# Three more places for expert weights, another order of places, eight PSUM banks for the second half, four row blocks stored by halves

## The chip, the cores and the metric

The kernel runs on one core of a Trainium2 chip. The metric is the device time of one execution in microseconds (us). TensorE (PE) does the matrix products, VectorE (DVE) and ScalarE (ACT) empty PSUM, GpSimd (POOL) does a few element-wise steps, and SyncE (SP) issues every DMA, in one in-order queue.

## The reference, cut to what matters

Three stages in float32: attention over 32 memory slots, a layer that takes the maximum of three products, and a soft mixture of eight experts. Only the last one is touched by the change. Its inputs are the 4608 rows `x` of 512 columns that the second stage leaves.

```python
logits = x @ phi                       # 4608 x 32 slots
d = softmax(logits, axis=0)            # over the rows
slot_input = (d.T @ x).reshape(E, 4, 512)
for e in range(E):                     # E = 8 experts
    h = maximum(slot_input[e] @ w1[e], 0)     # w1[e]: 512 x 1024
    slot_out[e] = h @ w2[e]                   # w2[e]: 1024 x 512
c = softmax(logits, axis=1)            # over the 32 slots
return c @ slot_out.reshape(32, 512)   # 4608 x 512
```

## The kernel before

**The stages.** The list `ORDER` is a hand-written order in which the attention and the second stage of eight batches run, until about 387 us of the span. Then follow the last softmax over the rows and the slot inputs (until about 400 us), the experts' first weights (`ex_in`, from 399.7 us), the experts' second weights by column halves (`ex_out(e, 0)`, then `ex_out(e, 1)`), and the output rows (`st_out`).

**The expert weights.** The weights are cut into 64 pieces of 128 x 1024 floats, 512 KB each. `pieces` lists them in the order of their use: first weights of expert 0, first weights of expert 1, first-half second weights of expert 0, and so on; the last 16 pieces are the second-half second weights of the eight experts. Each piece goes to a *place* in SBUF; `slots` lists the places in the order in which memory comes free, and piece k goes to place k modulo `NSLOT`. `send(n)` issues the DMAs of the next n pieces on SP. Before, `NSLOT` is 41. The first 34 places are spare memory and memory that the attention frees. Three more (`more2`) come free when `main_x` closes at the end of `ORDER`, one in `hbuf` after the last slot sums, three in `wo` after the last product with it. The 23 pieces that are left go to the first 23 places again: `ex_in` and `ex_out` call `send(1)` after each piece that they have used. A place can also be a list of four parts of 256 columns (`mix`), which are loaded by four DMAs of 128 KB.

**The output rows.** There are nine row blocks: block r below 8 holds the first 512 rows of batch r, block 8 the 64 last rows of every batch. `st_out(r, x)` computes columns 256x to 256x+255 of a block: twelve products into four PSUM banks `ts[0..3]`, then four copies to SBUF, two by ACT and two by DVE. The banks come from `mx()`, the pool `x` of four banks; `ps_m` has three further banks and `ps_l` one. First halves (x = 0) run between the `ex_out(e, 1)`, second halves (x = 1) at the end, in the order 0 to 5, 8, 6, 7. The number `NH` decides how a block is stored. Block r below `NH` is stored by halves: each half has a place of its own and one DMA of 512 KB, whose runs in DRAM are 1 KB. The other blocks have two places, both halves are gathered there, and only after the second half two DMAs of 512 KB with runs of 2 KB store them (four of 256 KB from 64 partitions each for block 8). Before, `NH` is 6.

**The DMAs' order.** SP issues the reloads first, in the order of the pieces, and the stores after them, in the order of `st_out`. Each DMA also waits for the one eight places ahead of it in the queue (eight semaphores serve in turn).

**Names.** L286 and L284 are the two `dma_start` lines of `send` (whole piece, part of a piece), L1016 the products of `ex_in`, L1033 those of `ex_out`, L1082 and L1086 those of `st_out`, L1095 and L1093 its copies on ACT and DVE, L1106 the store of a half block, L1099 that of two quarters of a whole block, L1104 that of block 8.

Of the kernel before, what the change touches and what calls it, by code (L numbers as in the profile page):

```python
# [7 lines left out]
FP32 = mybir.dt.float32  # L8
# [17 lines left out]
PIECE = 1024  # L26
NX = 6
# [133 lines left out]
LL = 0  # L161
VP = 3
EXTRA = 2
NSLOT = EXTRA + 9 + 12 + NX + 2 + 3 + 3 + 1 + 3


@with_exitstack
def kernel(
# [18 lines left out]
    ps_m = ctx.enter_context(tc.tile_pool(name="ps_m", bufs=3, space=PSUM))  # L187
    ps_l = ctx.enter_context(tc.tile_pool(name="ps_l", bufs=1, space=PSUM))
# [12 lines left out]
    def bank(pool, tag):  # L201
        return pool.tile([128, 512], FP32, tag=tag, name=tag)

    def mx():
        return bank(ps_x, "x")


    arena = keep.tile([128, (9 + 12 + NX) * PIECE], FP32, name="arena")
# [6 lines left out]
    s_run = keep.tile([128, FF], FP32, name="s_run")  # L215
    stat = keep.tile([128, 2], FP32, name="stat")
    h5x = keep.tile([128, 1920], FP32, name="h5x")
# [6 lines left out]
    hbuf = keep.tile([128, 3, 1536], FP32, name="hbuf")  # L224
# [17 lines left out]
    x0 = a0 + 12288  # L242
# [13 lines left out]
    slots = [extra[:, PIECE * j:PIECE * j + PIECE] for j in range(EXTRA)]  # L256
    slots += [arena[:, o:o + PIECE] for o in slot_off]
    late_slots = [h5x[:, 0:PIECE]] + [arena[:, PIECE * j:PIECE * j + PIECE] for j in range(9)]
    late_slots += [hbuf[:, 2, 0:PIECE], arena[:, x0:x0 + PIECE]]

    order = [("in", 0)]
    for e in range(E):
# [8 lines left out]
    def slot(k):  # L271
        return slots[k % NSLOT]

# [4 lines left out]
    def send(n):  # L278
        for _ in range(n):
            if sent[0] < len(pieces):  # L280
                x = slot(sent[0])
                if isinstance(x, list):
                    for g in range(4):
                        nc.sync.dma_start(out=x[g], in_=pieces[sent[0]][:, 256 * g:256 * g + 256])  # L284
                else:
                    nc.sync.dma_start(out=x, in_=pieces[sent[0]])  # L286
                sent[0] += 1
# [418 lines left out]
    def st_exp(t, rows, key):  # L706
        nm = pair.tile([128, 4], FP32, tag="nm", name="nm")
        rs = slice(0, rows)
        nc.vector.tensor_reduce(out=nm[rs, 0:1], in_=t[rs, 0:128], axis=AX.X, op=ALU.max)
        nc.vector.tensor_scalar(  # L710
            out=nm[rs, 2:3], in0=nm[rs, 0:1], scalar1=stat[rs, 0:1], scalar2=-1.0, op0=ALU.max, op1=ALU.mult)
        nc.vector.tensor_tensor(out=nm[rs, 1:2], in0=stat[rs, 0:1], in1=nm[rs, 2:3], op=ALU.add)
        nc.vector.tensor_scalar(out=stat[rs, 0:1], in0=nm[rs, 2:3], scalar1=-1.0, scalar2=None, op0=ALU.mult)
        dt = pair.tile([128, 128], FP32, tag="dt", name="dt")
        sm = pair.tile([128, 4], FP32, tag="sm", name="sm")
        o, x = dt[rs], t[rs, 0:128]
        if 1 < key < B - 1:
            o, x = o.rearrange("p (t a) -> p a t", a=4), x.rearrange("p (a t) -> p a t", a=4)
        nc.scalar.activation(out=o, in_=x, func=ACTF.Exp, bias=nm[rs, 2:3], accum_out=sm[rs, 1:2])
        nc.scalar.activation(out=sm[rs, 0:1], in_=nm[rs, 1:2], func=ACTF.Exp)  # L720
        nc.vector.scalar_tensor_tensor(
            out=stat[rs, 1:2], in0=stat[rs, 1:2], scalar=sm[rs, 0:1], in1=sm[rs, 1:2],
            op0=ALU.mult, op1=ALU.add)
        nc.scalar.activation(out=lt_all[rs, key], in_=t[rs, 0:128], func=ACTF.Copy)
        dtok[key] = (dt, sm)
# [70 lines left out]
    def warm(n, late=False):  # L796
        if n < 1:
            return
        t = bank(ps_m, "m") if late else bank(ps_l, "l")
        for _ in range(n):  # L800
            nc.tensor.matmul(t[:, 0:128], ident, ident, start=True, stop=True)  # L801
# [5 lines left out]
    with tc.manual_schedule():  # L807
# [5 lines left out]
        def late_slots_in():  # L813
# [19 lines left out]
            send=send, rl=rest_logit, rx=lambda: st_exp(lg["r"], 96, 8), rtm=rest_tm, rtc=rest_tc,  # L833
# [4 lines left out]
        for x in ORDER.split(";"):  # L838
            x = x.split()
# [2 lines left out]

        main_x.close()
        more2 = ctx.enter_context(tc.tile_pool(name="more2", bufs=1, side="right"))
        more2_sb = more2.tile([128, 3 * PIECE], FP32, name="more2")
        slots.extend(more2_sb[:, PIECE * j:PIECE * j + PIECE] for j in range(3))
        send(3)
        L = B - 1
        st_logit(L, 5)
        last_logit(LL, 6)  # L850
# [62 lines left out]
        for x in range(2):  # L913
            y = mx()
            for i in range(3):
                nc.tensor.matmul(
                    y[:, 32 * i:32 * i + 32], s_run[:, 128 * (3 * x + i):128 * (3 * x + i) + 128], wsel,
                    start=True, stop=True)
            if x:
                nc.vector.tensor_copy(out=st[x], in_=y[:, 0:96])  # L920
            else:
                nc.scalar.activation(out=st[x], in_=y[:, 0:96], func=ACTF.Copy)
        nc.vector.memset(msk, 0.0)
        warm(W[2], True)
        seen = set()
# [136 lines left out]
        ov = out.rearrange("(g x s) c -> x s g c", x=2, s=S)  # L1062
        free = [slots[64 - NSLOT + j] for j in range(NSLOT - (64 - NSLOT))]
        free = [x for x in free if not isinstance(x, list)]

        NH = 6
        tok = {}
        for r in range(9):
            tok[r] = [free.pop(0) for _ in range(1 if r < NH else 2)]

        def st_out(r, x):
            cs = slice(256 * x, 256 * x + 256)
            whole = r >= NH
            if not whole and x == 1 and free:
                tok[r] = [free.pop(0)]
            ts = [mx() for _ in range(4)]
            for k, (c, o) in enumerate(((ch, sh), (cl, sh), (ch, sl))):
                for g in range(4):
                    if r == 8 and g == 3:
                        continue  # L1080
                    rs = slice(32 * g, 32 * g + 32)
                    nc.tensor.matmul(  # L1082
                        ts[g][:, 0:256], c[rs, r], o[rs, cs], start=(k == 0), stop=(k == 2), tile_position=(32 * g, 0))
            if r == 8:
                for k, (c, o) in enumerate(((ch, sh), (cl, sh), (ch, sl))):
                    nc.tensor.matmul(ts[3][:, 0:256], c[:, 9], o[:, cs], start=(k == 0), stop=(k == 2))  # L1086
            for g in range(4):
                if whole:
                    o = tok[r][g // 2].rearrange("p (g c) -> p g c", g=2)[:, g % 2, cs]
                else:  # L1090
                    o = tok[r][0].rearrange("p (g c) -> p g c", g=4)[:, g]
                if g % 2:
                    nc.vector.tensor_copy(out=o, in_=ts[g][:, 0:256])  # L1093
                else:
                    nc.scalar.activation(out=o, in_=ts[g][:, 0:256], func=ACTF.Copy)  # L1095
                if whole and x == 1 and g % 2:
                    o = tok[r][g // 2].rearrange("p (g c) -> p g c", g=2)
                    if r < 8:
                        nc.sync.dma_start(  # L1099
                            out=out[S * r + 128 * g - 128:S * r + 128 * g + 128].rearrange("(g p) c -> p g c", p=128),  # L1100
                            in_=o)
                    else:
                        for y in range(2):
                            nc.sync.dma_start(out=ov[y, 512:576, g - 1:g + 1], in_=o[64 * y:64 * y + 64])  # L1104
            if not whole:
                nc.sync.dma_start(  # L1106
                    out=out[S * r:S * r + 512, cs].rearrange("(g p) c -> p g c", p=128),
                    in_=tok[r][0].rearrange("p (g c) -> p g c", g=4))
# [3 lines left out]
        for r in range(9):  # L1112
            if r < E:
                ex_out(r, 1)
            if r == E - 1:
                so_a(1)
            if r == E:
                so_b(1)
            st_out(r, 0)
        for r in [0, 1, 2, 3, 4, 5, 8, 6, 7]:  # L1120
            st_out(r, 1)
# [59 lines left out]
```

## Time and profile before

| | us |
|---|---|
| time before, median of 3 runs | 465.71 (465.19 to 467.65) |
| the profiled execution, its own time | 465.06 |
| its span, from the first to the last instruction | 463.3 |
| PE busy / DVE / ACT / POOL | 439.9 / 328.5 / 192.6 / 70.8 |
| DMA | 109.49 MB, mean 236 GB/s |

The times below are counted from the span's start. A busy share is an average over stages with different limits, so the table says little by itself: what matters for this change is the stretch from about 365 us to the end, and there the second part of the page (40 slices of 11.6 us) tells for each slice how busy the DMA engines were, how many GB/s they moved, and which clock TensorE was granted.

### The profile page before, as it was taken

To read this page: it belongs to the slowest core of one execution; us is meant where nothing else is said; L and a number is where in the kernel's file an instruction comes from. 1 tells how busy PE (TensorE), PEld (TensorE's weight loads), DVE (VectorE), ACT (ScalarE), POOL (GpSimd) and SP (SyncE) were. 2 spreads that over 40 slices of the span, in tenths; PEclk is the share of its full clock that TensorE was granted. 3 is DMA by queue.
4 is the path that set the end of the run, shared out by engine and by line. 5 is a ranking of instruction groups with operands and counts; after the bars stand their busy time and mean duration, and the time that the engine had idled before them with its cause. 6 is when DMAs were issued, how large, how long until landed. Compare 5 with 4: busy or idle time off the path is not lost.

```text
span 463.3 us, 12581 instructions
## 1 busy us (share of the span) xinstructions
PE 439.9 (95%) x5233; PEld 363.4 (78%) x5233; DVE 328.5 (71%) x753; ACT 192.6 (42%) x450; POOL 70.8 (15%) x92
## 2 busy tenths in 40 slices
PE   6999999999999999999999999998999989999981
PEld 5788899888997888888979879887878886654561
DVE  2397998767787968898679878999464434595541
ACT  3468768542544334243233433444333222133431
POOL 1137436421110011002100200112000000011000
PEclk9999999999999999999999999999999999999955
DMA  8967677558026137546368447779719905899988
GB/s 306 393 262 322 219 276 253 217 172 348 1 77 241 47 133 285 160 163 215 120 198 358 130 141 244 277 297 316 235 44 355 369 3 190 317 409 407 383 299 273
DMA packets 47657, 109.49 MB, mean 236 GB/s; under 512 B 3440, under 2 KB 26224, under 8 KB 45552
## 3 DMA queue, kind: packets, MB, share of 16 engines
q1 hardware_dynamic: 47600, 108.69, 64.8%
q8 instruction: 41, 0.67, 0.6%
q14 instruction: 16, 0.13, 0.1%
HBM read 91.38 MB, written 17.30 MB: 235 GB/s over the span
## 4 chain that ended last, share of the span: by engine, by line
PE 87%; DVE 4%; DMA 3%; ACT 2%; issue 1%; SPq 0%; DVEq 0%; ACTq 0%
PE m L597 49%; PE x L564 7%; PE l L801 5%; PE x L439 3%; PE x L1082 3%; PE x L748 2%; PE l L680 2%; PE x L475 2%; PE m L1016 2%; PE m L1033 2%; PE x L639 2%; DMA hbuf<-tr 2%; PE x L343 1%; PE l L1033 1%; DMA tr<-arena 1%
## 5 line engine op out<-in xcount | busy, mean ns | idle before, releaser
L597 PE MATMUL m<-ah,vh 128*128 128x288 f32 x576 | 171.2, 312 | 2.1 <-ACT g L607 1.5
L597 PE MATMUL m<-ah,vl 128*128 128x288 f32 x576 | 161.7, 296 | 0.0
L597 PEld LDWEIGHTS m<-ah,vh 128*128 128x128 f32 x576 | 108.3, 188 | 22.1 <-issue 9.4
L597 PE MATMUL m<-al,vh 128*128 128x288 f32 x576 | 123.3, 295 | 0.0
L597 PEld LDWEIGHTS m<-ah,vl 128*128 128x128 f32 x576 | 108.6, 188 | 0.2
L597 PEld LDWEIGHTS m<-al,vh 128*128 128x128 f32 x576 | 92.4, 188 | 0.1
L607 ACT ACTIVATE g<-m 128x288 f32<-128x288 f32 x96 | 38.9, 411 | 80.2 <-PE m L597 69.7
L609 DVE TENSOR_TENSOR g<-m,g 128x288 f32<-128x288 f32 x96 | 42.7, 450 | 33.0 <-PE m L597 22.4
L573 ACT ACTIVATE vh<-x 128x384 fp32r<-128x384 f32 (+1 forms) x100 | 42.0, 478 | 49.5 <-PE x L564 37.6
L611 DVE TENSOR_TENSOR ht<-m,g 128x288 f32<-128x288 f32 x96 | 42.7, 451 | 18.6 <-PE m L597 7.2
L579 DVE TENSOR_TENSOR vl<-x,vh 128x384 fp32r<-128x384 f32 (+1 forms) x100 | 48.8, 531 | 8.9 <-ACT vh L573 8.5
L532 POOL TENSOR_TENSOR al<-arena,ah 128x576 fp32r<-128x576 f32 x16 | 23.7, 1483 | 107.5 <-ACT ah L528 105.0
L564 PE MATMUL x<-arena,kvt 64*32 64x384 f32 (+1 forms) x800 | 39.3, 477 | 0.4 <-ACT vh L573 0.4
L325 POOL TENSOR_TENSOR arena<-arena 128x768 uint32<-128x768 uint32 (+1 forms) x13 | 23.4, 1804 | 39.5 <-ACT arena L313 14.5
L801 PE MATMUL l<-cst 128*128 128x128 f32 x162 | 25.3, 305 | 3.9 <-DMA cst<-in_consts_dram 3.2
L801 PEld LDWEIGHTS l<-cst 128*128 128x128 f32 x162 | 21.6, 208 | 7.3 <-DMA cst<-in_consts_dram 3.2
L564 PEld LDWEIGHTS x<-arena,kvt 64*32 64x32 f32 x800 | 12.0, 106 | 13.0 <-issue 8.1
L643 DVE STREAM_TRANSPOSE arena<-ht 128x512 f32<-128x512 f32 x30 | 20.7, 697 | 0.5 <-DMA tr<-arena 0.3
L439 PE MATMUL x<-arena 128*32 128x129 f32 x640 | 19.4, 274 | 0.2 <-ACT arena L402 0.2
L439 PEld LDWEIGHTS x<-arena 128*32 128x32 f32 x640 | 17.3, 110 | 2.9 <-ACT arena L402 0.9
L616 POOL COPY arena<-ht 128x64 f32<-128x64 f32 x24 | 5.2, 238 | 76.3 <-DVE ht L611 76.3
L528 ACT ACTIVATE ah<-arena 128x576 fp32r<-128x576 f32 x16 | 11.0, 684 | 11.2 <-DVE arena L518 11.2
(246 smaller groups left out, 587.3 us busy)
## 6 DMA issues: line engine op xcount, KB each, us to landing
arena<-in_e_w_dram SPq DMA_DIRECT2D x44, 512.0 KB, 7.5
arena<-in_w_dram SPq DMA_DIRECT2D x14, 768.0 KB, 6.0
arena<-in_kv_dram SPq DMA_DIRECT2D x8, 1290.0 KB, 9.5
arena<-in_q_dram SPq DMA_DIRECT2D x16, 576.0 KB, 7.0
arena<-in_kv_dram SPq DMA_DIRECT2D x8, 1032.0 KB, 8.1
tr<-arena SPq DMA_DIRECT2D x30, 256.0 KB, 3.0
hbuf<-tr SPq DMA_DIRECT2D x30, 256.0 KB, 4.3
arena<-in_phi_t_dram SPq DMA_DIRECT2D x8, 576.0 KB, 5.7
```

The costliest lines, as they stand in the source:

```text
L325: (eng or nc.gpsimd).tensor_tensor(out=du, in0=du, in1=lo.bitcast(U32), op=ALU.add)
L439: nc.tensor.matmul(t[32 * g:32 * g + 32, 0:KVC], phin_sb[:, j, b, 32 * g:32 * g + 32], kv_sb[:, j, b, g] if j < 4 else kv4_sb[:, g], start ...
L532: nc.gpsimd.tensor_tensor(out=al[n][:, :, c], in0=aT_sb[:, :, c], in1=ah[n][:, :, c].bitcast(FP32), op=ALU.subtract)
L564: nc.tensor.matmul(t[b][32 * g:32 * g + 32, 128 * r0:128 * r1], kvt[n][r, b, 32 * g:32 * g + 32], w_sb[r, i, r0:r1, g], start=True, stop=T ...
L573: nc.scalar.activation(out=v1[n, i][0][:, b, c], in_=ph["v1", n, i][b][:, c], func=ACTF.Copy)
L579: nc.vector.tensor_tensor(out=vl[:, b, c], in0=ph["v1", n, i][b][:, c], in1=vh[:, b, c].bitcast(FP32), op=ALU.subtract)
L597: nc.tensor.matmul(t[:, 0:HALF], x, y, start=(k == 0), stop=(k == 5))
L607: nc.scalar.activation(out=g1[u, hf], in_=t[:, 0:HALF], func=ACTF.Copy)
L609: nc.vector.tensor_tensor(out=g1[u, hf], in0=t[:, 0:HALF], in1=g1[u, hf], op=ALU.max)
L611: nc.vector.tensor_tensor(out=ht[n, i][:, cs], in0=t[:, 0:HALF], in1=g1.pop((u, hf)), op=ALU.max)
L643: nc.vector.transpose(out=v, in_=ht[n, i][:, 0:512])
L801: nc.tensor.matmul(t[:, 0:128], ident, ident, start=True, stop=True)
```

## The change

- `more2` has five places in place of three, and `send(5)` follows in place of `send(3)`.
- A new place in four parts, `s_run[:, 512:768]` and three parts of `h5x`, is appended after the slot inputs are computed, with a `send(1)`. `NSLOT` is 44.
- The two last of the `late_slots` change their order: `arena[:, x0:...]` now stands before `hbuf[:, 2, ...]`.
- In the second half (x = 1) the odd blocks 1, 3, 5, 7 take the three banks of `ps_m` and the one of `ps_l`; the even ones keep the four of `mx()`.
- `NH` is 4 in place of 6.

```diff
-NSLOT = EXTRA + 9 + 12 + NX + 2 + 3 + 3 + 1 + 3
+NSLOT = EXTRA + 9 + 12 + NX + 2 + 3 + 5 + 2 + 3
...
-    late_slots += [hbuf[:, 2, 0:PIECE], arena[:, x0:x0 + PIECE]]
+    late_slots += [arena[:, x0:x0 + PIECE], hbuf[:, 2, 0:PIECE]]
...
-        more2_sb = more2.tile([128, 3 * PIECE], FP32, name="more2")
-        slots.extend(more2_sb[:, PIECE * j:PIECE * j + PIECE] for j in range(3))
-        send(3)
+        more2_sb = more2.tile([128, 5 * PIECE], FP32, name="more2")
+        slots.extend(more2_sb[:, PIECE * j:PIECE * j + PIECE] for j in range(5))
+        send(5)
...
+        slots.append([s_run[:, 512:768]] + [h5x[:, PIECE + 256 * j:PIECE + 256 * j + 256] for j in range(3)])
+        send(1)
         nc.vector.memset(msk, 0.0)
...
-        NH = 6
+        NH = 4
...
-            ts = [mx() for _ in range(4)]
+            if x == 1 and r % 2:
+                ts = [bank(ps_m, "m") for _ in range(3)] + [bank(ps_l, "l")]
+            else:
+                ts = [mx() for _ in range(4)]
```

SP's queue from the last loads of `ORDER` (about 363 us before) to the first reloads (400 us): `-` is before, `+` is after. `arena`, `hbuf`, `more_5414` (this is `more2`), `s_run`, `h5x`, `wo` and `extra` are the memories in which the places lie.

```order
-L286 DMA arena<-in_e_w_dram 128x1024 x3
+L286 DMA arena<-in_e_w_dram 128x1024 x4
 L286 DMA hbuf<-in_e_w_dram 128x1024
-L286 DMA arena<-in_e_w_dram 128x1024
-L286 DMA more_5414<-in_e_w_dram 128x1024 x3
+L286 DMA more_5414<-in_e_w_dram 128x1024 x5
 L286 DMA hbuf<-in_e_w_dram 128x1024
+L284 DMA s_run<-in_e_w_dram 128x256
+L284 DMA h5x<-in_e_w_dram 128x256 x3
 L286 DMA wo<-in_e_w_dram 128x1024 x3
```

One `arena` load moved ahead of the `hbuf` load that waits, two loads to `more2` and one in four parts are new ahead of `wo`; the reloads behind are three fewer.

SP's queue behind the last reload, before:

```order
L1106 DMA out_dram<-arena 128x4x256 x6
L1106 DMA out_dram<-more_5414 128x4x256 x2
L1106 DMA out_dram<-hbuf 128x4x256
L1106 DMA out_dram<-wo 128x4x256 x3
L1104 DMA out_dram<-arena 64x2x512 x2
L1104 DMA out_dram<-more_5414 64x2x512 x2
L1099 DMA out_dram<-arena 128x2x512 x3
L1099 DMA out_dram<-hbuf 128x2x512
```

And now (L1111 is the store of a half block, L1104 of two quarters, L1109 of block 8):

```order
L1111 DMA out_dram<-more 128x4x256
L1111 DMA out_dram<-h5x 128x4x256
L1111 DMA out_dram<-arena 128x4x256 x2
L1111 DMA out_dram<-more_5414 128x4x256 x4
L1104 DMA out_dram<-arena 128x2x512 x4
L1109 DMA out_dram<-hbuf 64x2x512 x2
L1109 DMA out_dram<-more_5414 64x2x512 x2
L1104 DMA out_dram<-arena 128x2x512 x4
```

Six first-half stores have become four; blocks 4 and 5 are stored whole, by four DMAs ahead of block 8.

TensorE's queue for the second half of block 1, before (`x` is a bank of `mx()`, `sh`/`sl` and `ch`/`cl` the two parts of the slot outputs and of the softmax):

```order
L1082 MATMUL x<-sh,ch 128x256 [waits Activation_49]
L1082 MATMUL x<-sh,ch 128x256 [waits DVE_49]
L1082 MATMUL x<-sh,ch 128x256 [waits Activation_49]
L1082 MATMUL x<-sh,ch 128x256 [waits DVE_49]
L1082 MATMUL x<-sh,cl 128x256 x4
L1082 MATMUL x<-sl,ch 128x256 x4
```

And now (L1087 is the same line, `m` and `l` are banks of `ps_m` and `ps_l`):

```order
L1087 MATMUL m<-sh,ch 128x256 [waits PE_49] x3
L1087 MATMUL l<-sh,ch 128x256
L1087 MATMUL m<-sh,cl 128x256 x3
L1087 MATMUL l<-sh,cl 128x256
L1087 MATMUL m<-sl,ch 128x256 x3
L1087 MATMUL l<-sl,ch 128x256
```

The waits for ACT's and DVE's copies of the block before are gone; from block 2 on each block waits for the copies of the block two before it, except block 6, which follows block 8 on the same four banks.

## Rows read from the trace of the kernel before

**Rows 1.** The page's second part: 40 slices of 11.6 us, DMA share in tenths, GB/s.

```profile
DMA  8967677558026137546368447779719905899988
GB/s 306 393 262 322 219 276 253 217 172 348 1 77 241 47 133 285 160 163 215 120 198 358 130 141 244 277 297 316 235 44 355 369 3 190 317 409 407 383 299 273
```

**Rows 2.** Busy times by stretch; the last three columns are clock, DMA share, GB/s.

```profile
372.00:386.00 14.00, 12.46 (x100) 11.26 (x103) 5.11 (x12) 3.23 (x8) 0.83 (x4) 1.00 0.00 1
388.00:396.00 8.00, 7.15 (x126) 4.66 (x128) 3.75 (x15) 1.77 (x7) 0.00 (x0) 1.00 0.96 350
396.00:399.00 3.00, 3.00 (x38) 2.24 (x32) 2.06 (x3) 0.38 (x1) 0.00 (x0) 1.00 0.61 183
399.00:432.00 33.00, 31.48 (x549) 17.56 (x548) 22.68 (x62) 10.48 (x28) 3.50 (x4) 1.00 1.02 401
432.00:434.60 2.60, 2.60 (x52) 1.54 (x51) 1.01 (x3) 0.95 (x4) 0.00 (x0) 1.00 1.10 381
```

**Rows 3.** SP's issues in order of time: start, duration, line, count.

```profile
363.44 2.34 SPq L286 DMA_DIRECT2D arena<-in_e_w_dram  x3
386.49 0.33 SPq L286 DMA_DIRECT2D hbuf<-in_e_w_dram  x1
386.86 0.43 SPq L286 DMA_DIRECT2D arena<-in_e_w_dram  x1
387.90 1.28 SPq L286 DMA_DIRECT2D more<-in_e_w_dram  x3
393.60 0.33 SPq L286 DMA_DIRECT2D hbuf<-in_e_w_dram  x1
396.77 1.28 SPq L286 DMA_DIRECT2D wo<-in_e_w_dram  x3
428.15 0.33 SPq L284 DMA_DIRECT2D more<-in_e_w_dram  x1
440.78 2.05 SPq L1106 DMA_DIRECT2D out_dram<-more  x2
```

**Rows 4.** What TensorE waited for from 399 to 440 us, the longest of five.

```profile
PE l L1033 <- DVE hbuf L1025: 0.9, 2, 0.5
```

**Rows 5.** TensorE's weight loads of the last piece's four parts, and a first-half copy.

```profile
434.46 0.11 PEld L1033 LDWEIGHTS m<-kvt,hbuf 128*32 128x32 f32 x1
434.64 0.10 PEld L1033 LDWEIGHTS m<-more,hbuf 128*32 128x32 f32 x1
...
424.97 0.66 ACT L1095 ACTIVATE arena<-x 128x256 f32<-128x256 f32 x2 [1.16 <-PE x L1082]
```

**Rows 6.** The chain that ended last, second half of blocks 0 and 1, and its end.

```profile
439.07 0.85 PE x L1082 x8
440.30 0.04 issue
440.34 1.25 PE x L1082 x11
441.60 0.38 ACT more L1095
...
454.45 0.33 DVEq L1177
```

**Rows 7.** Stretches of the stores, columns as in rows 2.

```profile
436.00:440.00 4.00, 3.13 (x26) 2.04 (x26) 1.89 (x6) 1.65 (x6) 0.00 (x0) 0.88 1.09 385
440.00:441.50 1.50, 1.23 (x13) 1.12 (x12) 0.70 (x2) 0.57 (x2) 0.00 (x0) 0.50 0.52 182
441.50:454.50 13.00, 11.05 (x89) 8.29 (x84) 5.86 (x16) 5.11 (x16) 0.00 (x0) 0.50 0.96 306
452.00:453.50 1.50, 1.23 (x16) 0.94 (x12) 0.76 (x2) 0.66 (x2) 0.00 (x0) 0.50 0.97 222
457.00:460.50 3.50, 0.00 (x0) 0.00 (x0) 0.00 (x0) 0.00 (x0) 0.00 (x0) 0.50 1.04 397
461.50:462.00 0.50, 0.00 (x0) 0.00 (x0) 0.00 (x0) 0.00 (x0) 0.00 (x0) 0.50 0.20 78
```

## The prediction

> **What bounds the kernel now.** I read the page's 40 slices first. DMA is nearly still in slice 33 (3 GB/s) and then full or nearly full to the end [rows 1], so the end is a question of bytes and of when they may move. I cut that part finer. From 372 to 386 us DMA moves nothing; from 388 to 396 it moves 350 GB/s, from 396 to 399 only 183, then 401 GB/s until 432 [rows 2]. SP's issues say why: a load of `hbuf` waits until 386.5 us for its memory, an `arena` load stands behind it, the three of `more2` follow at 387.9, the next at 393.6 and 396.8 [rows 3]. Memory, not bandwidth, holds the loads back there.
>
> Does TensorE wait for these loads? In its list of waits from 399 to 440 us no DMA stands; the longest of the five lines is 0.9 us, for DVE [rows 4]. One trace of a load is to be found: of the last piece's four parts three start at 434.46 us and the fourth at 434.64 [rows 5]. So the weights arrive just in time at the very end, and late loads cost 0.2 us.
>
> What ends last? The second halves start at 439.07 us. A block takes 1.25 us of products, 0.38 us in which TensorE waits for ACT to empty the bank, and 0.04 us: 1.68 us, the ninth done at 454.45 [rows 6]. The stores follow at 306 GB/s, the pace at which blocks are made (512 KB in 1.68 us is 312). After 457 us only stores are left, at 397 GB/s; they fade out at about 461.8 us [rows 7]. So until 454 the blocks set the pace, and then a backlog of stores drains.
>
> **The change part by part.** A piece or a half block is 128 x 1024 x 4 bytes, 0.524 MB. I use the profiled execution: 465.06 us, span 463.3, last data at 461.8. The median is 0.65 us higher; differences are carried over to it.
>
> *Loads.* Thirty-two pieces are loaded after 386 us. One (`arena`) now stands ahead of the waiting `hbuf` load and follows the last loads of 363.4 to 365.8 us [rows 3] into the still stretch: 1.3 us of DMA leave the crowd. The two new places of `more2` are issued right behind the three of 387.9, whose five issues end by about 390; the next in the queue waits until 393.6 anyway, so nothing is held up on SP. The place in four parts waits for the last products with `s_run`, at about 395.8 us, and its four issues of 0.33 us or a little more stand ahead of `wo`. They delay `wo`'s issue of 396.77 by up to 0.9 us, which the DMA backlog of that moment covers: 6 pieces from 388, 1 from 393.6 and 1 from 395.8 keep DMA busy until about 398.5. So the stream is full from 388 us, and 31 pieces, 16.25 MB at 401 GB/s, end at 428.5 us, where before they ended at 432 to 434.6 [rows 2]. On TensorE this is worth the 0.2 us of rows 5, no more, because it did not wait elsewhere.
>
> The four parts of 128 KB: while the old four-part place was loaded, beside stores, DMA moved 381 GB/s [rows 2]. I cost them at nothing. The Trainium skill (SBUF — State Buffer, "The DMA setup-cost knee") gives each transfer about 2 us plus its bytes at 436 GB/s; as an estimate from that page, four parts one after another would take 9.2 us in place of 1.3, the loads would end at about 436.4, TensorE would be held by 1.8 us and the time would be about 467.1. This trace disagrees: the transfers overlap, at 381 GB/s.
>
> *First halves.* Stores of four blocks are left in place of six. Block 0's copy ends at 425.6 us [rows 5], the others 1.56 us apart; 2.10 MB at 385 GB/s, the rate of half-block stores in 436 to 440 us [rows 7], end at about 434.0. From there DMA is idle until the first second-half store moves, at about 441.5 us (issue 440.78 [rows 3]). That is 7.5 us, in which before it was busy until about 440. What the loads win is therefore not kept: the two stores taken out here, 1.05 MB, come at the end instead.
>
> *Second halves.* Odd blocks have banks of their own, so the 0.38 us waits go (but for block 6 behind block 8) and a block takes some 1.25 us: 419 GB/s of half blocks, above the 385 that their stores reach. ACT's two copies, 0.66 us [rows 5], fit beside. So from block 0 on DMA is the bound, with 14 half blocks, 7.34 MB, where before 12 stood there. Without the extra banks the four half blocks would be paced at 1.68 us, 1.3 us more, and the later blocks, stored whole, would outrun DMA even then: the eight banks are worth 1.3 us here at most.
>
> *The sum from 441.5 us.* Blocks 0 to 3, 2.10 MB at 385: 5.4 us. Blocks 4 and 5, 2.10 MB at 397: 5.3. Block 8, 1.05 MB: its stores are from 64 partitions each, and in 452 to 453.5 us, when they ran, DMA was 97% busy and moved 222 GB/s [rows 7]; that gives 4.7 us, the rate of the other whole stores 2.6. I take 3.7, between, since the four now queue behind full ones and can overlap. Blocks 6 and 7: 5.3. The fading out: 0.4. Together 441.5 + 20.1 = 461.6, against 461.8. With the 0.2 us of TensorE the change gives 0.4 us: 464.7 for the profiled execution, **465.3** on the median.
>
> On block 8 the Trainium skill (SBUF — State Buffer, "Door 1: the DMA port swizzle") says that 64 neighbouring partitions reach only 8 of 16 ports, some 218 GB/s. The 222 GB/s agree. By that rule alone block 8 takes 4.8 us, as an estimate, and the time is 466.4: a rule against a queue in which block 8 stands in the middle of a full stream.
>
> Ends: with block 8 at 2.6 us and a fade of 0.2 the sum is 460.1 with TensorE's gain, 1.7 us better. With the first four blocks at the old pace (6.7 us), the whole ones at 385 GB/s (11.0), block 8 at 4.7 and a fade of 0.7 it is 464.6, 2.8 us worse. All the bad ends together are unlikely.
>
> **The rivals.** *Faster: the stores run better than any single row.* TensorE waits less in the second half, so it may be granted 2.4 GHz again where rows 7 show 0.50; all blocks would then be queued by about 447 us. With block 8 hidden (2.6) and whole stores at the 401 GB/s of the loads instead of 397, the end comes 1.8 to 2.5 us sooner: 463.2 to 463.9. For it: a longer backlog leaves DMA no gaps between stores. Against it: half-block stores never passed 385 in the stretches I looked at, and DMA, not TensorE, is the bound.
>
> *Slower: the second-half stores stay at the 306 GB/s of 441.5 to 454.5 us.* The row can be read as a limit of DMA, since its share is 0.96 there. Then 7.34 MB take 24.0 us, the end is at 465.9 with the fade, 4.1 us later: 469.8. It decides for slower from a mean below about 325 GB/s over the tail. Against it: 385 in 436 to 440 us with the same half-block stores, and 512 KB in 1.68 us explains 306 by itself.
>
> *The change doesn't do what it says:* the new places fill no sooner, since SP issues in order and some load waits longer than I think. The loads then end at 432 as before, TensorE still does not wait, and what is left is the second halves: 465.3 to 465.7.
>
> **How the numbers follow.** Forecast 0.60, faster rival 0.16, slower rival 0.14, no earlier loads 0.10. A measurement of this kernel tells about 0.5% (2.3 us) from no change. Faster by more than that takes three quarters of the first rival and 0.02 of the forecast's low end: 0.14. Slower takes the second rival and 0.02 of the forecast's high end: 0.16. The rest, 0.70, is within 0.5%. The range goes from 463.4, which takes in half of the faster rival, to 467.8, which takes in block 8 at half rate and a slower start of the second half but not the 306 GB/s rival: about 2 in 10 are left out.
>
> **What would show it.** Right: DMA at 390 GB/s or more from 388 us on without the dip at 396; last load landed near 428; DMA idle between about 434 and 441.5; blocks of the second half 1.25 to 1.3 us apart, done near 451; no compute from there, and 10 us of stores alone at about 390 GB/s; the end within 1 us of before. Wrong: a second half that starts earlier than 438.5 us; stores in the tail below 325 or above 410 GB/s; stores still running at 440 us, which would mean that the loads did not end early; a wait of TensorE for the part loads near 417 us, where the new place's piece is used.

## The result and the profile after

The changed kernel took 468.02 us, the median of 12 runs (465.66 to 470.68). The kernel before, measured beside it, took 464.81 us (464.23 to 471.29). The ratio is 1.0058, 95% interval 1.0031 to 1.0085: slower, with an interval that does not reach 1. The forecast was 465.3 us, no change, and its range ended at 467.8.

The profiled execution took 468.82 us; its span is 467.0 us, against 463.3 before. First the slices, as in [rows 1] (40 slices, now of 11.7 us):

```profile
DMA  8959576649016137546359446779609905999598
GB/s 318 373 206 373 177 310 219 251 155 362 1 57 257 47 124 283 166 160 215 119 194 370 127 166 206 280 290 309 247 38 366 387 10 198 358 412 408 208 351 280
```

In slice 38 (208 GB/s; counted from 1, as the prediction counts its slice 33) DMA now stands still for a while, where before it moved 383. Next the stretches to the end, with the columns of [rows 2] and [rows 7] (times of PE, PEld, DVE, ACT, POOL with counts, granted clock, DMA share, GB/s):

```profile
390.40:392.40 2.00, 2.00 (x67) 1.84 (x67) 1.11 (x5) 0.53 (x3) 0.00 (x0) 1.00 0.86 260
392.40:394.40 2.00, 1.83 (x23) 0.70 (x24) 0.73 (x5) 0.99 (x4) 0.00 (x0) 1.00 0.83 315
...
396.40:398.40 2.00, 1.78 (x18) 1.66 (x21) 0.91 (x3) 0.25 (x1) 0.00 (x0) 1.00 1.01 406
398.40:400.40 2.00, 2.00 (x28) 1.24 (x23) 1.62 (x2) 0.38 (x1) 0.00 (x0) 1.00 0.99 392
400.40:402.40 2.00, 2.00 (x24) 1.79 (x27) 0.87 (x4) 0.26 (x1) 0.00 (x0) 1.00 0.85 288
402.40:406.40 4.00, 4.00 (x80) 2.45 (x76) 1.67 (x4) 0.79 (x3) 0.00 (x0) 1.00 0.94 337
...
434.40:438.40 4.00, 3.84 (x72) 2.09 (x68) 2.03 (x6) 1.45 (x5) 0.00 (x0) 1.00 0.98 341
438.40:442.40 4.00, 3.12 (x38) 2.08 (x38) 2.18 (x7) 1.95 (x7) 0.00 (x0) 1.00 0.10 35
...
443.40:449.90 6.50, 6.50 (x77) 5.51 (x71) 4.57 (x14) 4.03 (x13) 0.00 (x0) 0.50 0.94 308
449.90:455.30 5.40, 0.05 (x1) 0.00 (x0) 0.70 (x3) 0.54 (x2) 0.00 (x0) 0.50 1.04 382
455.30:459.70 4.40, 0.00 (x0) 0.00 (x0) 0.00 (x0) 0.00 (x0) 0.00 (x0) 0.50 0.94 283
459.70:465.20 5.50, 0.00 (x0) 0.00 (x0) 0.00 (x0) 0.00 (x0) 0.00 (x0) 0.50 0.99 370
```

From 438.4 to 442.4 us DMA is 10% busy. Then 7.34 MB of stores take 21.8 us. The last four rows divide this tail by its rates: the four half blocks at 308 GB/s, blocks 4 and 5 at 382, block 8 with some bytes of its neighbours at 283, blocks 6 and 7 at 370 with the fading out. In the first microsecond of the half blocks the queue only fills, and what follows is still below 385:

```profile
443.40:444.40 1.00, 1.00 (x23) 1.00 (x18) 0.83 (x4) 0.69 (x3) 0.00 (x0) 0.50 0.66 209
444.40:449.90 5.50, 5.50 (x61) 4.51 (x58) 3.74 (x11) 3.33 (x11) 0.00 (x0) 0.50 0.99 326
```

From the chain of waits, as in [rows 6], the start of the second halves and the end of all products and copies:

```profile
441.48 0.61 PE x L1087 x9
...
450.26 0.33 DVEq L1182
```

TensorE is done 4.2 us sooner than in [rows 6], although `ex_in` began 2.4 us later, and nothing is won by it: DMA was late already.

How much of the 3.7 us between the two spans belongs to the change? The first products with the experts' weights (`ex_in`, on the place `extra`) start here, before and after (duration in ns, first and last start):

```profile
L1016 PE MATMUL m<-extra,p x16: 378/379/404, 399.7 to 400.4; 128*32 128x256 f32 x16
```

```profile
L1018 PE MATMUL m<-extra,p x16: 379/379/403, 402.1 to 402.8; 128*32 128x256 f32 x16
```

In this profile 2.4 us lie ahead of `ex_in`, where the two programs differ by a few loads issued after 363 us and nothing else. From `ex_in` to the end of the span it is 63.6 us before and 64.9 now: 1.3 us. This second number is the measure for the experiments; the last section shows what the 2.4 us are.

### The profile page after: what moved, and what is told of

It reads as the page before. It is cut to its first block, busy times and chain, and to the rows that moved or that the text cites. A ratio compares the mean times of both kernels' runs of the same rounds, so it can differ in the third digit from the quotient of the medians.

```text
span 467.0 us, 12577 instructions
## 1 busy us (share of the span) xinstructions
PE 437.0 (94%) x5233; PEld 361.7 (77%) x5233; DVE 328.1 (70%) x753; ACT 192.5 (41%) x450; POOL 70.8 (15%) x92
## 4 chain that ended last, share of the span: by engine, by line
PE 83%; DVE 7%; DMA 4%; ACT 2%; issue 1%; SPq 0%; DVEq 0%; ACTq 0%
PE m L597 46%; PE x L564 7%; PE l L801 6%; PE x L439 3%; PE x L748 2%; PE l L680 2%; PE x L1087 2%; PE m L1018 2%; PE m L1035 2%; PE x L475 2%; PE x L639 2%; DMA hbuf<-tr 2%; DMA tr<-arena 1%; PE x L343 1%; PE l L1035 1%
## 5 line engine op out<-in xcount | busy, mean ns | idle before, releaser
L801 PE MATMUL l<-cst 128*128 128x128 f32 x162 | 26.9, 317 | 3.9 <-DMA cst<-in_consts_dram 3.3
L801 PEld LDWEIGHTS l<-cst 128*128 128x128 f32 x162 | 23.0, 220 | 7.6 <-PE l L801 3.4
```

## Experiments

One table for all runs, in us: the first `ex_in` and the span of the profiled execution, their difference (the time from `ex_in` to the end), and the timed ratio to the kernel before. The runs were made on several chips; each ratio is to the kernel before on the same chip.

| run | first `ex_in` | span | difference | ratio, 95% interval |
|---|---|---|---|---|
| before | 399.7 | 463.3 | 63.6 | |
| b_again | 399.1 | 462.1 | 63.0 | 0.9976 (0.9948 to 1.0004) |
| b_third | 402.3 | 465.7 | 63.4 | 0.999 (0.996 to 1.0019) |
| after | 402.1 | 467.0 | 64.9 | 1.0058 (1.0031 to 1.0085) |
| a_again | 401.9 | 466.6 | 64.7 | 1.0049 (1.0022 to 1.0075) |
| a_third | 401.1 | 465.6 | 64.5 | 1.0028 (0.9992 to 1.0064) |
| b_nh4 | 399.7 | 465.1 | 65.4 | 1.0036 (1.0003 to 1.0069) |
| b_places | 399.6 | 462.1 | 62.5 | 0.9999 (0.9968 to 1.0031) |
| b_banks | 400.2 | 462.1 | 61.9 | 1.0011 (0.9979 to 1.0043) |
| b_banks_nh8 | 401.5 | 463.7 | 62.2 | 0.9958 (0.9924 to 0.9992) |
| a_nh6 | 401.7 | 464.3 | 62.6 | 0.9996 (0.9966 to 1.0025) |
| a_nh8 | 399.1 | 459.3 | 60.2 | 0.9943 (0.991 to 0.9977) |
| nh8_again | 402.1 | 462.1 | 60.0 | 0.9936 (0.9899 to 0.9974) |
| nh8_il | 402.5 | 460.9 | 58.4 | 0.9881 (0.983 to 0.9931) |
| nh8_swap | 399.3 | 458.9 | 59.6 | one run, no ratio |
| nh8_two | 406.1 | 467.7 | 61.6 | 1.0002 (0.9966 to 1.0038) |
| a_64 | 400.1 | 468.9 | 68.8 | one run, no ratio |
| a_b8 | 403.7 | 486.4 | 82.7 | 1.042 (1.0376 to 1.0464) |

The three profiles of one program differ by up to 0.6 us in the difference column, and by up to 3.2 us in the column of `ex_in`.

**The two programs again (b_again, a_again, b_third, a_third).** No edit.

> The kernel before once more, unchanged, for a second profile of it. Theory 'gap' (the loss of the change lies at its end: the stores of two first halves left a stretch in which DMA then stands still and went behind it): 464.8 us, 63.5 us from the first product of ex_in to the end of the span, as in the first profile; the start of ex_in may differ by up to 2 us between executions of the same program, since in the profiles TensorE's products before 15 us took 266 ns each until 9 us in one and until 12 us in the other. Rival 'start' (the changed program is slower before its changed part begins): the first ex_in again within 0.3 us of 399.8 us.

> The changed kernel once more, unchanged. Theory 'gap': 64.8 us from the first ex_in to the end again, and a start of ex_in anywhere between 399.5 and 402.5 us; time 1.3 us above the kernel before, plus or minus 1. Rival 'start': ex_in again at 402.2 us, time 3 us above.

> The kernel before for the third time. Theory 'chance': 63.0 to 63.5 us from the first ex_in to the end, ex_in anywhere between 399 and 404 us. Rival 'program': ex_in below 400.3 us again.

> The changed kernel for the third time. Theory 'chance' (what its times have above the 1.5 us of the tail comes from two places ahead of the changed part that differ from execution to execution: the step of TensorE's clock near 8 to 12 us and the wait for the transposing transfer near 323 us): 64.8 us from the first ex_in to the end again, the ratio between 1.001 and 1.006 and not the same as the 1.0058 and 1.0049 of the first two. Rival 'program' (the changed program is slower there too): ex_in at 401.5 us or later again and a ratio of 1.005 or more.

Before is 63.3 us in the mean of three, after 64.7: the change costs 1.4 us (0.3%) in the part that it touches. `ex_in` of the unchanged kernel came at 402.3 us in the third profile, later than in any of the three of the changed one; the rival "program" falls. The ratios of the changed kernel went from 1.0058 to 1.0049 and 1.0028. Each interval holds the 1.003 of the profiles or ends at it, but the mean of the three is 1.0045: the medians of the two repeats differ from the kernel before by 2.0 and 1.9 us. That chance makes up the half microsecond above 1.4 is likely and not shown.

**How many blocks by halves (a_nh6, a_nh8, b_nh4).** The edit of a_nh6; a_nh8 has 8 there, and b_nh4 is the kernel before with 4 in place of its 6.

```diff
-        NH = 4
+        NH = 6
```

> The changed kernel with NH = 6: new places and eight banks stay, blocks 4 and 5 are stored by halves again. Theory 'gap': their first halves fill the still stretch from 439.5 to 443 us, 1.05 MB leave the tail, at 385 GB/s 2.7 us: 62.1 us from the first ex_in to the end, time 463.4 us, some 1.4 us faster than the kernel before. Rival 'stores' (1 KB runs hold the half-block stores at some 330 GB/s wherever they stand beside copies): the tail has 12 half blocks at 330 in place of 8, 4 of them in place of whole ones at 390: the gain is 2.7 less 1.0 us, 63.1 us and 464.4. Rival 'start': 465.5 or more, since ex_in begins at 402 us.

> The changed kernel with NH = 8: all of blocks 0 to 7 by halves. Theory 'gap': eight first halves end at about 442.1 us (counted with ex_in at 399.8), just when the second halves' first store may move; 4.19 MB at 385 GB/s, block 8 at 222 to 397, 0.4 of fading: end at 456.0 to 458.1, 57.7 to 59.8 us from the first ex_in, time 459.1 to 461.1. Rival 'stores': 4.19 MB at 330 GB/s are 12.7 us, end at 457.8 to 459.9, 461 to 463 us. Rival 'start': 2.4 us above the first.

> The kernel before with NH = 4 alone. From the first ex_in to the end of the span the kernel before took 63.5 and 63.0 us in two profiles, the changed one 64.8 twice. Theory 'gap' (two first-half stores moved behind a stretch in which DMA stands still): first-half stores end near 437 instead of 440 us, the tail carries 1.05 MB more: four half blocks paced at 1.68 us, then 5.4 + 4.4 + 5.4 us of whole blocks: 65.0 to 65.5 us, and 1.9 us more in time than the kernel before. Rival 'banks' (the eight banks let the stores bunch, and that costs): NH = 4 alone changes little, 63.0 to 63.8.

From NH = 4 to 6 the changed kernel gains 2.1 us (64.7 to 62.6), halfway between the 62.1 of "gap" and the 63.1 of "stores"; from 6 to 4 the kernel before loses 2.1 (63.3 to 65.4), as "gap" said. The timed ratios agree: 1.0049 falls to 0.9996, and b_nh4 is at 1.0036. So the one number explains more than the whole loss, in either surrounding, and "banks" falls. In a_nh6 the two first halves fill about half of the hole, up to some 441 us:

```profile
438.00:440.00 2.00, 1.26 (x12) 0.73 (x12) 1.20 (x4) 1.32 (x5) 0.00 (x0) 1.00 1.06 373
440.00:442.00 2.00, 1.80 (x27) 1.36 (x27) 0.99 (x3) 0.63 (x4) 0.00 (x0) 1.00 0.49 174
```

In b_nh4 the hole is there without any of the other edits:

```profile
436.00:438.00 2.00, 1.25 (x11) 0.72 (x11) 1.17 (x4) 1.33 (x5) 0.00 (x0) 1.00 0.86 303
438.00:440.00 2.00, 1.55 (x15) 1.01 (x15) 0.98 (x4) 0.62 (x3) 0.00 (x0) 1.00 0.18 64
440.00:442.00 2.00, 1.54 (x14) 1.25 (x14) 1.07 (x4) 0.98 (x4) 0.00 (x0) 0.57 0.24 84
```

NH = 8 closes the hole and is 0.6% faster than the kernel before (0.9943 and 0.9936). At 60.2 us it stayed 0.4 above the range that "gap" gave and at the upper end of that of "stores" (60.1), and its rows say why: first halves at 384 GB/s, second halves at 339 beside copies and 359 when the copies are over.

```profile
436.00:440.00 4.00, 3.41 (x45) 2.32 (x44) 2.18 (x7) 1.98 (x7) 0.00 (x0) 1.00 1.09 384
442.00:446.00 4.00, 3.14 (x47) 2.45 (x46) 3.23 (x10) 2.95 (x10) 0.00 (x0) 1.00 1.01 339
446.00:450.00 4.00, 0.00 (x0) 0.00 (x0) 0.22 (x1) 0.00 (x0) 0.00 (x0) 0.76 1.06 359
```

**One part alone (b_places, b_banks, b_banks_nh8).** b_places is the kernel before with `NSLOT` 44, the three new places and the other order; b_banks has only the banks; b_banks_nh8 has the banks and NH = 8.

```diff
-            ts = [mx() for _ in range(4)]
+            if x == 1 and r % 2:
+                ts = [bank(ps_m, "m") for _ in range(3)] + [bank(ps_l, "l")]
+            else:
+                ts = [mx() for _ in range(4)]
```

> The kernel before with the new places and their order alone (NSLOT 44, NH = 6, four banks). Theory 'gap': loads and first-half stores end some 2 to 3 us earlier and DMA waits for the second halves, which start when they did: 63.0 to 63.5 us from the first ex_in, no change in time. Rival: the four parts or the load moved ahead in the queue cost something: 64 us or more.

> The kernel before with the eight banks alone (NH = 6). Theory 'gap': TensorE no longer waits 0.38 us a block, six half blocks leave at the pace of DMA: 62.4 to 62.8 us, 0.4 to 1.0 us faster. Rival 'banks': 64 us or more. If DMA alone set the pace before, 63.3 and no change.

> The kernel before with the eight banks and NH = 8, without the new places. Theory 'room' (the new places pay only when first-half stores fill the stretch that they free): loads and eight first-half stores keep DMA busy until 443 to 445 us, so the second halves' stores begin 2 to 3 us later than with the places: 62.2 to 63.2 us from the first ex_in (60.2 with the places), no faster than the kernel before. If the places are worth nothing: 60.2 us, and 2.5 to 3 us faster than before.

The places alone gain 0.8 us and the banks alone 1.4, both more than expected. Two profiles of one program differ by up to 0.6, and the timed ratios, 0.9999 and 1.0011, show neither gain. Both together, in a_nh6, gain 0.7: they don't add up. With NH = 8 the places are worth 2.1 us (62.2 to 60.1), as "room" said; but "no faster than the kernel before" was not met, since b_banks_nh8 is at 0.9958. The timed ratios with and without the places (0.994 and 0.9958) lie closer together than the profiles, and their intervals overlap, so the size of this gain is less certain than its direction. Without the places DMA is still full when the second halves want to start:

```profile
438.00:440.00 2.00, 1.54 (x19) 0.80 (x17) 1.18 (x3) 0.66 (x2) 0.00 (x0) 1.00 1.09 384
440.00:442.00 2.00, 1.48 (x15) 0.94 (x15) 1.17 (x3) 1.04 (x3) 0.00 (x0) 1.00 1.07 372
```

**Why block 8 is slow (a_64, a_b8, nh8_two, nh8_il).** In a_64 the whole stores of blocks 4 to 7 are split as block 8's are:

```diff
-                        nc.sync.dma_start(out=out[...].rearrange("(g p) c -> p g c", p=128), in_=o)
+                        ow = out[...].rearrange("(g p) c -> p g c", p=128)
+                        for y in range(2):
+                            nc.sync.dma_start(out=ow[64 * y:64 * y + 64], in_=o[64 * y:64 * y + 64])
```

> The changed kernel (NH = 4) with each of the eight stores of blocks 4 to 7 split into two of 64 partitions; rows and 2 KB runs in DRAM stay as they were. Their 4.19 MB took 10.8 us. Theory 'partitions': 240 to 300 GB/s, as block 8's, so 14.0 to 17.5 us: 68.0 to 71.5 us from the first ex_in to the end (64.8 without). Rival 'rows': 64.6 to 65.3, no more than the extra issues cost.

```profile
453.00:457.00 4.00, 0.00 (x0) 0.00 (x0) 0.00 (x0) 0.00 (x0) 0.00 (x0) 0.50 0.85 280
457.00:465.00 8.00, 0.00 (x0) 0.00 (x0) 0.00 (x0) 0.00 (x0) 0.00 (x0) 0.50 0.86 268
```

268 to 280 GB/s where the same bytes went at 370 to 382. The edit changes two things, the partitions that a store reads and its size (256 KB in place of 512); nh8_il below has stores of 256 KB that read 128 partitions. a_b8 was to show the reverse on block 8:

```diff
-                            nc.sync.dma_start(out=ov[y, 512:576, g - 1:g + 1], in_=o[64 * y:64 * y + 64])
+                            nc.sync.dma_start(out=ov[:, 512:576, g - 1 + y], in_=o[:, y])
```

> The changed kernel with block 8 stored by four DMAs of 128 partitions and one row group each, in place of four of 64 partitions and two row groups; bytes, 2 KB runs and the number of DMAs stay. Theory 'ports' (block 8 goes at 240 to 300 GB/s because one DMA reads 64 partitions): its 1.05 MB take 2.7 us in place of 4.4: 63.1 us from the first ex_in (64.8 without), 1.7 us faster than the changed kernel. Rival 'rows' (its rows lie in eight groups of 64, far apart in DRAM, and that slows it): 64.6 to 64.9, no change.

It lost 18 us by another mechanism and told nothing on partitions. While its four stores ran, the DMA share was 0.13, that of 2 of the 16 engines, and they moved 50 GB/s.

```profile
460.00:464.00 4.00, 0.00 (x0) 0.00 (x0) 0.00 (x0) 0.00 (x0) 0.00 (x0) 0.50 0.13 50
464.00:468.00 4.00, 0.00 (x0) 0.00 (x0) 0.00 (x0) 0.00 (x0) 0.00 (x0) 0.50 0.13 51
```

The outermost dimension of its pattern in DRAM counts 2, where it counts 64 or 128 in the other stores. The Trainium skill (DMA: Bandwidth & Descriptors, "Rules for kernel authors") says that the number of engines follows the slowest dimension that is not 1; these rows agree.

nh8_two is the changed kernel with NH = 8; it keeps the shape of block 8's stores and gives the upper 64 partitions a queue of their own, that of ACT:

```diff
-                        for y in range(2):
-                            nc.sync.dma_start(...)
+                        for y, q in enumerate((nc.sync, nc.scalar)):
+                            q.dma_start(...)
```

> The changed kernel with NH = 8, and of block 8's four stores of 64 partitions the two of the upper partitions are issued by ACT on a queue of its own, the two of the lower ones by SP as before. With NH = 8 alone block 8's stores ran from about 450 to 454.5 us (1.05 MB in 4.3 us), 60.2 us from the first ex_in to the end. Theory 'partitions' (a store that reads 64 partitions alone is slow, and one queue takes the two one after the other): both halves are read at once, block 8 takes 2.7 us, 58.6 us, time 461.4. Rival 'rows' (its rows lie in eight groups of 64 in DRAM): 60.0 to 60.4, time 463.

No gain: 61.6 us, 1.5 more than with one queue (60.1). From 453 to 461 us, where block 8's stores and the last half blocks ran together, DMA was full and moved 304 GB/s.

```profile
453.00:461.00 8.00, 0.25 (x5) 0.00 (x0) 1.23 (x4) 1.21 (x4) 0.00 (x0) 0.50 1.03 304
```

This run decides nothing between the theories, because the two halves were not read at once. ACT's queue (q10) moved 0.50 MB of its 0.52 from 453 to 459 us (first line: packets, MB, share of the engines' time) and the rest from 459 to 464 (second line):

```profile
q10 hardware_dynamic: 276, 0.50, 39.0%
q10 hardware_dynamic: 12, 0.02, 1.7%
```

SP's half of block 8 stood behind half blocks in SP's queue, and its packets (of 2 KB, those of half blocks are of 1 KB) began to move only at 459 us. Besides, the two issues on ACT, of 1.08 and 0.90 us, stood among its copies of block 6 and delayed them. nh8_il is the cleaner test, with NH = 8, one queue, 64 as the outermost count and all 128 partitions in each store; for this the columns of block 8's softmax are written in another order, so that neighbouring partitions alternate between the two groups of rows:

```diff
...
+            if x0 >= 8:
+                src = src[:, 0].rearrange("p (x s) -> p x s", x=2)
+                h, l = (a[:, x0].rearrange("p (s x) -> p x s", x=2) for a in (ch, cl))
...
-                            nc.sync.dma_start(out=ov[y, 512:576, g - 1:g + 1], in_=o[64 * y:64 * y + 64])
+                            nc.sync.dma_start(out=ov[:, 512:576, g - 1 + y].rearrange("x s c -> s x c"), in_=o[:, y])
```

> The changed kernel with NH = 8, and block 8's rows interleaved: the columns of ch and cl for block 8 are written in the order (s, x) in place of (x, s), so that each of its four stores reads all 128 partitions and its outermost run in DRAM still counts 64. Theory 'partitions': its 1.05 MB go at about 385 GB/s, 2.7 us in place of 4.3: 58.6 us from the first ex_in to the end (60.2 without), time 1.6 us below NH = 8 alone. Rival 'rows' (the eight groups of 64 rows far apart in DRAM): 60.0 to 60.4.

> The changed kernel with NH = 8 once more, to stand beside the interleaved one on the same chip: 60.2 us from the first ex_in to the end; 0.9943 of the kernel before, give or take 0.003.

58.4 us against 60.0 on the same chip, as expected; the rows in DRAM are the same, so "rows" falls, and the stores are of 256 KB as in a_64, so their size was not it either. The intervals of the two timed ratios (0.9881 and 0.9936) overlap; the stretch of block 8 shows the cause, without and with the edit:

```profile
453.00:457.00 4.00, 0.00 (x0) 0.00 (x0) 0.00 (x0) 0.00 (x0) 0.00 (x0) 0.50 0.94 280
```

```profile
453.00:456.00 3.00, 0.00 (x0) 0.00 (x0) 0.00 (x0) 0.00 (x0) 0.00 (x0) 0.50 1.05 383
```

This is the fastest version of the study: 0.9881 of the kernel before, 462.05 us.

**Why the second halves' stores are slower (nh8_swap).** With NH = 8 the two halves write each other's columns:

```diff
-                nc.sync.dma_start(out=out[S * r:S * r + 512, cs]...
+                nc.sync.dma_start(out=out[S * r:S * r + 512, 256 - 256 * x:512 - 256 * x]...
```

> The changed kernel with NH = 8 in which the stores of the two halves write each other's columns (the first half to columns 256 to 511, the second to 0 to 255), so the output is not the reference's; everything else stays. With NH = 8 the first halves' stores ran at 383 GB/s (436 to 440 us), the second halves' at 333 to 363 (442 to 450). Theory 'place in DRAM' (the second KB of each 2 KB row is written more slowly): the rates change places, first below 365, second about 383. Rival 'what runs beside': first 383, second 333 to 363 as before, 60.2 us from the first ex_in.

```profile
436.00:440.00 4.00, 3.40 (x41) 2.31 (x41) 2.18 (x7) 1.95 (x7) 0.00 (x0) 1.00 1.09 385
442.00:446.00 4.00, 3.36 (x51) 2.65 (x47) 3.23 (x10) 2.93 (x10) 0.00 (x0) 1.00 1.05 357
446.00:450.00 4.00, 0.00 (x0) 0.00 (x0) 0.43 (x2) 0.19 (x1) 0.00 (x0) 0.70 1.06 363
```

First halves at 385 and second at 357 to 363, as with the columns in place: the place in DRAM is not it. Nor is TensorE's clock, which is 1.00 in 442 to 446 us. What runs beside can't be all of it, since 363 stays when the copies are over. Why these stores don't reach 385 is left open.

## Why the prediction was wrong, step by step

*What bounds the kernel: right.* No DMA wait of TensorE matters; the second halves start 39.4 us after `ex_in` in both profiles. The 0.2 us that earlier loads were to bring on TensorE did not come.

*Loads and first halves: right in kind, wrong in size, and of no consequence.* The dip at 396 us is gone (406 and 392 GB/s), but the stream that was to be full from its start begins with 260 and 315, and a new dip follows while the part loads run (288 and 337), where four part loads were costed at nothing. With everything 2.4 us later in this profile, the stores were to end at 436.4 us and ended near 438.4; after that DMA stands still until 443.4. The sentence "what the loads win is therefore not kept: the two stores taken out here come at the end" was the right mechanism, and NH = 6 and 4 in four kernels show it to be worth 2.1 us. So the rival of no earlier loads is out too.

*Second halves: right in kind, and TensorE faster than forecast.* Blocks no longer wait for their bank, all are done at 450.26 us, 8.8 us after the start in place of 15.4, and DMA is the bound from the first block on. The forecast had kept the 1.25 us of products of [rows 6] for each block, some 12 us in all; it is 0.98 us a block, with a granted clock of 0.50 from 443.4 us on. This changed nothing, since DMA was slower still.

*The sum of the tail: here the prediction failed.* It put 20.1 us, and 21.8 were measured. In the table the bytes of each term are divided by the rate of its stretch; the stretches themselves don't end where a block ends (that of block 8 lasted 4.4 us and moved 1.25 MB, where block 8 has 1.05).

| term | predicted | at the measured rate |
|---|---|---|
| blocks 0 to 3, by halves, 2.10 MB | 5.4 | 6.8 (308 GB/s) |
| blocks 4 and 5, whole, 2.10 MB | 5.3 | 5.5 (382 GB/s) |
| block 8, 1.05 MB | 3.7 | 3.7 (283 GB/s) |
| blocks 6 and 7 with the fading out, 2.10 MB | 5.7 | 5.7 (370 GB/s) |

The mis-sized term is the first, 1.4 of the 1.7 us. It took 385 GB/s from first-half stores [rows 7] for second-half stores. The nearer row was 306 GB/s of 441.5 to 454.5 us, which was explained away by the pace of the blocks. That pace was indeed gone, and yet 308 (316 in a_again) remained; for this part of the tail the slower rival was right. About a third of the 1.4 us is the queue that fills in the first microsecond (209 GB/s at a share of 0.66), which the sum did not have. The rest is a rate of 326 with DMA full (a share of 0.99); in the NH = 8 runs it is 339 to 363. Why it is not 385 the runs leave open, as the experiment on the two halves' columns says. The forecast's "bad end" for this term, 6.7 us, came in full, by another way than the pace that was named for it. The first store's start 0.5 us sooner gave some back.

The block 8 term was right in size, in part by luck. The middle between 222 and 397 GB/s was taken because its stores could overlap with full ones in the queue. 283 is what came, but a_64 has 268 to 280 where only stores of 64 partitions stand in the queue, so full ones beside them are not needed for it. What block 8 loses against 383 GB/s, some 1.0 us, a_64 and nh8_il put down to the 64 partitions. The rule of the Trainium skill on block 8 (SBUF — State Buffer, "Door 1: the DMA port swizzle") gave 466.4 us; the 283 here and the 268 to 280 GB/s of a_64 are above its 218 and far below the full rate.

*The rivals.* The slower rival was to decide from a mean below 325 GB/s over the tail; 7.34 MB in 21.8 us are 337. The faster rival needed TensorE at 2.4 GHz again. In a_third it came half true: from 442.4 us the granted clock was 0.86 in the mean, and the stores of this stretch went at 318 GB/s all the same, with 64.5 us from `ex_in` to the end.

```profile
442.40:448.90 6.50, 5.32 (x81) 4.44 (x74) 5.10 (x15) 4.40 (x14) 0.00 (x0) 0.86 0.97 318
```

So the part that was changed lost 1.4 us, 0.3%, where 0.4 us of gain was forecast. The measured 0.58% has this and most likely the chance of the last section in it. The range had room for a slow block 8 but not for both.

## What to carry to other kernels

Work that filled a hole in the transfer queue cost nothing here, and the same work behind the hole cost its time: when loads are made to end sooner, give the freed stretch more stores, not fewer (from `ex_in` on, the changed kernel with NH = 8 gained 3.2 us on the kernel before, with NH = 4 it lost 1.4). Price a transfer by the row with the same source, run length and surroundings, and where that row has another explanation, keep its rate until an experiment removes the explanation. In a store, look at the partitions that it reads and at the count of its outermost dimension before its bytes: 64 neighbouring partitions cost 27 to 30% of the rate here, and an outermost count of 2 cost 87%.

## What the runs showed of the hardware that was not expected

All programs of this study run the same instructions up to about 363 us, and still `ex_in` starts anywhere from 399.1 to 406.1 us. Nearly all of it arises at two places, with a few tenths more between 250 and 300 us; from 330 us to `ex_in` all eighteen profiles keep their distance within 0.05 us, so the loads that the change moved cost nothing ahead of `ex_in`. The first place is the start. TensorE runs dummy products (L801) there; at some moment eight of them take 1.17 us in place of 2.09, and that moment differs between executions. From the chains of before and of after:

```profile
9.17 0.50 PE l L801 x2
9.68 0.04 issue
9.72 1.17 PE l L801 x8
```

```profile
9.26 0.81 PE l L801 x2
10.07 0.04 issue
10.12 2.09 PE l L801 x8
```

The rows show 1.00 as granted clock on either side, so only the durations tell. In after it came some 3 us later than in before, and everything behind is 1.7 us later. The second place is at 323 us, where TensorE waits for a transfer (`hbuf<-tr`) that turns a matrix. From the timeline of b_again and of a_again, the product that waits (start, duration, and in brackets the wait):

```profile
324.30 0.85 PE L748 MATMUL x<-hbuf,dk 128*32 128x384 f32 x8 [1.40 <-DMA hbuf<-tr]
```

```profile
325.74 1.51 PE L748 MATMUL x<-hbuf,dk 128*32 128x384 f32 x8 [2.65 <-DMA hbuf<-tr]
```

The stretches behind it, of b_again and then of a_again (granted clock, DMA share and GB/s are the last columns):

```profile
325.00:327.00 2.00, 2.00 (x28) 1.29 (x25) 0.36 (x1) 0.88 (x3) 0.00 (x0) 1.00 0.99 341
```

```profile
325.00:327.00 2.00, 1.26 (x8) 0.23 (x8) 0.00 (x0) 0.00 (x0) 0.00 (x0) 0.54 1.02 399
327.00:329.00 2.00, 2.00 (x22) 0.59 (x19) 0.00 (x0) 0.14 (x1) 0.00 (x0) 0.61 0.97 380
```

After a wait of 1.40 us TensorE runs on at a granted clock of 1.00 (2.4 GHz); after 2.65 us it is granted 0.54, nearly the lower level of 1.2 GHz, and the eight products take 1.51 us in place of 0.85, the sixteen behind them 1.53 in place of 0.88. So 1.25 us of later landing become 2.5 us. Whoever compares kernels of this kind by a few tenths of a per cent should compare the part that was changed, in several profiles, beside the medians.
